# An explicit order of every engine's instructions, in place of a list scheduler, in a fused attention and spectral kernel

## The chip, the cores and the metric

The kernel runs on one core of a Trainium2 chip. The metric is device time in microseconds (us), lower is better. One program, one launch, bf16 inputs and outputs. A kernel's executions are said to be *fast* or *slow*: slow is one that took more than 1.5% longer than the fastest of the same kernel. Only fast ones enter the comparisons.

Engine names as the profile has them: PE is the matmul engine and PEld its weight loads, DVE the vector engine, ACT the scalar engine, POOL the GpSimd engine, SP the engine that issues most DMAs. "Busy" is the profile's word: matmuls overlap and their ends are modelled, so a busy PE is not PE at its peak.

## The reference, cut to what matters

Two branches over the same 2048 rows of 640, mixed by a gate per row:

```python
def _A_ref(x, wq, wk, wv, wo, beta):        # 32 heads of 20, 4 segments of 512 rows
    q, k, v = x @ wq, x @ wk, x @ wv        # split in heads and segments  [shortened]
    for s in range(4):
        p = softmax(qs @ ks.T * scale + mask)          # causal inside the segment
        a_dot = p @ vs
        a_mem = (phi(qs) @ M) / (phi(qs) @ z + 1e-06)  # memory of earlier segments
        outs.append(g * a_mem + (1 - g) * a_dot)
        M = M + phi(ks).T @ vs
        z = z + phi(ks).sum(rows)
    return concat(outs) @ wo
def _B_ref(x, w_r, w_i):
    return irfft2(rfft2(x) * (w_r + 1j * w_i))
g = sigmoid((x * gate_w).sum(-1))
out = g * A + (1 - g) * B                   # both branches on the same x
```

Both branches become matmuls in the kernel: the Fourier transforms are products with tables, and the second axis is folded first.

## The kernel before

The kernel records some 2350 operations with what they read and write, and each operation carries one or two *alternatives* (engine, function, cost, latency). Then a list scheduler runs a small clockwork of the chip on the host and decides the order in which each engine gets its instructions, and the PSUM bank that each result goes to.

The matmul helper and the evictions. All matmuls go through `mms`, so nearly all have the line number of that helper in the profile:

```python
def mms(self, items, r, w, prio, name="", extra=0.0):
    cost = sum(max(c * PECOL, 27.0) for _, c in items) + extra
    def f(e):
        for th, _ in items:
            o_, l_, r_, st, sp_, kw = th()
            h = e.matmul(o_, l_, r_, start=st, stop=sp_, **kw)
        return h
    return self.Sc.op({"pe": (f, cost, 110.0)}, r=r, w=w, prio=prio, name=name)

def either(self, fn, n, r, w, prio, name="", after=()):       # side work: DVE or POOL
    return self.Sc.op({"dve": (fn, 75 + 0.52 * n, 90.0), "pool": (fn, 100 + 1.95 * n, 90.0)}, ..., lock=True)
```

The score loop. The scores of four heads are four row-tiled matmuls that run at once in different rows of the array; they fill all four banks of the pool "qk", one exponential empties them, and only then may the next scores start. There are 80 such rounds:

```python
def qk_unit(self, s, pr, u, parts):
    bank = Bank(4, "qk")                     # the pool "qk" has 4 banks
    ...
        return (self.ps(bank, hh * 512 + o, [1, n]), kp.ap(..., p0=32 * hh, np_=DH),
                qp.ap(..., p0=32 * hh, np_=DH), True, True, {"tile_position": (32 * hh, 0)})
    ...
    self.one("act", lambda e: e.activation(dst(), src(), ACT.Exp, scale=SC), 4 * width, [bank], ...)
    # then a causal mask on POOL (affine_select), and 21-column matmuls of the probabilities with v
```

Three kinds of matmul stand in the stream: plain ones on the whole array; row-tiled scores as above; and column-tiled ones (`tile_position: (0, 32*q)`), which put four 32-column products side by side. Work beside the score loop (projections, the two transforms, memory reads, output projections) is what PE does while ACT is in an exponential.

The scheduler's heart, with cuts:

```python
def schedule(self, pools, plan=(), nsem=56):
    for o in ops if plan else ():            # PLAN: shifts of priorities, picks of alternatives
        shift, pick = divmod(plan[o.key], 3)
        o.prio += shift / 10.0
        ...
    def try_dispatch(e):                     # first ready operation by priority, banks free, not faster elsewhere
        ...
            if e == "pe":
                occ *= self.pe_slow(now, occ)
            if e == "dve" and o.lock:        # DVE and POOL share a port, in the model
                busy_until[e] = port = max(now, busy_until["pool"]) + occ
            if o.dma:                        # one number for the bandwidth of all transfers
                bw_free = max(bw_free + o.xfer, ...)
                o.t1 = bw_free + 2000.0 + lat
    while events: ...
```

The softmax here doesn't subtract the row's maximum and nothing guards it: scores larger than these inputs give would overflow.

## Time and profile before

254.12 us, median of three executions (253.64 to 255.82). The profiled execution took 255.64 us, near the top of that.

The exponentials of the kernel before: minimum, median and maximum duration in ns, the first and last start in us, then what ended ACT's idle time before them.

```profile
L1183 ACT ACTIVATE ex<-psum x80: 1857/1877/1966, 12.4 to 238.5; 128x2048 bf16<-128x2048 f32 x80
...
  PE psum L593: 17.3, 37
```

### The profile page before, as it was taken

What the parts mean: (1) busy time and instruction counts of PE and PEld (TensorE: products, weight loads), DVE (VectorE), ACT (ScalarE), POOL (GpSimd) and SP (SyncE); (2) the same over time, 40 slices, a digit from 0 to 9 for tenths busy, and PEclk for the clock granted to TensorE, in tenths of its full rate; (3) what the DMA queues carried; (4) which work ended last, traced back from release to release, by engine and by line L of the source; (5) the groups of instructions that cost most, each with busy time, mean ns of one, the idle gap of its engine ahead of it and who ended that gap; (6) DMA issues with size and microseconds to landing.
All of it is one profiled execution on the core that took longest, in us unless ns stands there. A gap on an engine that the chain in (4) does not pass through costs nothing.

```text
span 253.9 us, 7958 instructions
## 1 busy us (share of the span) xinstructions
PE 235.9 (93%) x3226; PEld 138.4 (55%) x3248; DVE 202.2 (80%) x556; ACT 203.1 (80%) x208; POOL 114.4 (45%) x175
## 2 busy tenths in 40 slices
PE   7999999989999989989989999999997999999993
PEld 2344556544665547644646566545563656456583
DVE  0789799759998899999999988979999984625543
ACT  2397499958999898999988889889889798788710
POOL 8004735523533336745255747535575532416400
PEclk9999999979999999999999999999999999999998
DMA  7997979599479366656238385313666303464223
GB/s 173 358 355 216 216 173 225 121 205 221 101 112 227 79 168 189 159 125 191 64 96 182 70 204 141 101 44 114 134 169 153 70 3 84 92 115 94 78 68 103
DMA packets 56003, 36.76 MB, mean 145 GB/s; under 512 B 31792, under 2 KB 52256, under 8 KB 55968
## 3 DMA queue, kind: packets, MB, share of 16 engines
q1 hardware_dynamic: 54272, 35.45, 57.6%
q10 hardware_dynamic: 1696, 0.82, 1.2%
q8 instruction: 25, 0.41, 0.7%
q14 instruction: 10, 0.08, 0.2%
HBM read 19.86 MB, written 9.84 MB: 117 GB/s over the span
## 4 chain that ended last, share of the span: by engine, by line
PE 57%; DVE 19%; DMA 10%; ACT 5%; SPq 3%; issue 3%; POOL 1%; ACTq 0%; DVEq 0%
PE psum L593 57%; ACT ex L1183 4%; DMA xsb<-in_A_x_dram 4%; DVE Pt L1333 3%; DMA pkn<-phk 3%; SPq L622 2%; DVE va L1089 2%; DVE xsb L913 1%; SPq L620 1%; DMA tt<-tab_tt 1%; DVE Cp L603 1%; DVE qu L603 1%; DVE xf L908 1%; DMA q_scr<-qu 1%; DMA Wt<-in_B_w_i_dram 1%
## 5 line engine op out<-in xcount | busy, mean ns | idle before, releaser
L1183 ACT ACTIVATE ex<-psum 128x2048 bf16<-128x2048 f32 x80 | 150.3, 1879 | 17.9 <-PE psum L593 17.3
L1186 POOL TENSOR_SCALAR_AFFINE_SELECT ex<-ex 128x512 bf16<-128x512 bf16 x128 | 80.7, 647 | 110.7 <-ACT ex L1183 109.3
L593 PEld LDWEIGHTS psum<-va,ex 128*128 128x128 bf16 x1280 | 36.6, 96 | 7.2 <-POOL ex L1186 2.5
L593 PE MATMUL psum<-va,ex 128*128 128x21 bf16 x1280 | 38.6, 173 | 1.7 <-POOL ex L1186 0.6
L593 PE MATMUL psum<-qp,kp 20*128 20x512 bf16 (+3 forms) x512 | 31.9, 303 | 1.5 <-ACT ex L1183 0.6
L593 PE MATMUL psum<-wv,xT 128*128 128x141 bf16 (+1 forms) x160 | 28.0, 306 | 1.5 <-DVE qu L603 0.6
L1333 DVE TENSOR_TENSOR Pt<-psum,Wt 128x642 bf16<-128x642 f32 x32 | 25.6, 822 | 2.7 <-PE psum L593 1.6
L593 PE MATMUL psum<-xT,wk 128*128 128x512 bf16 (+1 forms) x127 | 25.6, 384 | 2.1 <-DVE qu L603 0.8
L593 PE MATMUL psum<-xT,wq 128*128 128x512 bf16 (+1 forms) x132 | 26.5, 380 | 0.7 <-issue 0.4
L593 PE MATMUL psum<-wo,oT 128*128 128x320 bf16 x120 | 22.1, 301 | 0.0
L593 PEld LDWEIGHTS psum<-qp,kp 20*128 20x128 bf16 x512 | 9.0, 92 | 20.4 <-ACT ex L1183 10.7
L593 PEld LDWEIGHTS psum<-wv,xT 128*128 128x128 bf16 x160 | 13.0, 98 | 10.5 <-issue 1.2
L593 PE MATMUL psum<-big,Cp 128*128 128x321 bf16 (+1 forms) x96 | 17.2, 302 | 1.0 <-DVE eo L603 0.4
L1054 ACT ACTIVATE et<-qu 128x512 bf16<-128x512 bf16 x25 | 15.7, 635 | 2.5 <-DVE qu L603 2.4
L603 DVE CAST ot<-psum 128x320 bf16<-128x320 f32 x19 | 9.1, 490 | 10.6 <-PE psum L593 9.4
L1089 DVE TENSOR_TENSOR va<-psum,ebx 128x500 bf16<-128x500 f32 (+1 forms) x32 | 15.2, 482 | 2.8 <-PE psum L593 1.7
L593 PEld LDWEIGHTS psum<-xT,wk 128*128 128x128 bf16 (+1 forms) x140 | 9.7, 98 | 13.5 <-issue 2.7
L1379 DVE TENSOR_TENSOR G<-eo,psum 128x320 bf16<-128x320 f32 x32 | 14.7, 476 | 2.5 <-PE psum L593 2.4
L593 PEld LDWEIGHTS psum<-xT,wq 128*128 128x128 bf16 (+1 forms) x140 | 10.0, 97 | 11.3 <-issue 1.3
L1218 DVE TENSOR_TENSOR on<-psum,rs 128x320 bf16<-128x320 f32 x32 | 15.5, 483 | 0.3
L593 PE MATMUL psum<-big,Ac 128*128 128x161 bf16 (+2 forms) x96 | 14.5, 257 | 1.3 <-DVE qu L603 0.9
L593 PE MATMUL psum<-tt,Yt 128*128 128x256 bf16 (+1 forms) x96 | 15.0, 273 | 0.3
(80 smaller groups left out, 357.2 us busy)
## 6 DMA issues: line engine op xcount, KB each, us to landing
tt<-tab_tt SPq DMA_DIRECT2D x16, 256.0 KB, 2.9
xsb<-in_A_x_dram SPq DMA_DIRECT2D x8, 320.0 KB, 6.9
qp<-q_scr SPq DMA_DIRECT2D x28, 80.0 KB
kp<-k_scr SPq DMA_DIRECT2D x28, 80.0 KB
o_scr<-on SPq DMA_DIRECT2D x12, 160.0 KB
out_dram<-ot SPq DMA_DIRECT2D x12, 160.0 KB
q_scr<-qu SPq DMA_DIRECT2D x6, 256.0 KB
k_scr<-qu SPq DMA_DIRECT2D x6, 256.0 KB, 2.8
```

Source lines behind the costliest of these rows:

```text
L593: h = e.matmul(o_, l_, r_, start=st, stop=sp_, **kw)
L603: alts["dve"] = (lambda e: e.tensor_copy(dst(), src()), 75 + 1.04 * n, 85.0)
L620: return e.dma_start_transpose(d_, s_)
L622: return e.dma_start(d_, s_)
L908: self.either(lambda e, r=r, op=op: e.tensor_tensor(xf.ap(r * 642, [321, 2], [1, 320]), xs.ap(o, [D, 2], [1, 320]), xs.ap(o + 320, [D, 2], ...
L1054: self.one("act", lambda e: e.activation(et.ap(0, [1, L]), qsl(), ACT.Exp), L, [qb], [b("et", pi_)], late, name="phi_exp")
L1089: self.one("dve", lambda e: e.tensor_tensor(va.ap(i * H * VW + h0 * VW, [VW, nh], [1, DH]), self.ps(bank, 0, [DH, nh], [1, DH]), self.ebx. ...
L1183: self.one("act", lambda e: e.activation(dst(), src(), ACT.Exp, scale=SC), 4 * width, [bank], [self.exb(s, g, j) for g, j in outs], prio - ...
L1186: self.one("pool", lambda e, g=g, j=j: e.affine_select(self.ex.ap(self.exo(s, g) + JOFF[j], [1280, 4], [1, P]), self.ex.ap(self.exo(s, g) ...
L1218: self.one("dve", lambda e, rs=rs, bank=bank, g=g: e.tensor_tensor(on.ap(80 * g, [D, 4], [DH, 4], [1, DH]), self.ps(bank, 0, [88, 4], [VW, ...
L1333: self.one("dve", lambda e, ri=ri, Pt=Pt, Wt=Wt, bank=bank: e.tensor_tensor(Pt.ap(ri * 322, [644, 2], [1, KD]), self.ps(bank, 0, [0, 2], [ ...
L1379: self.one("dve", lambda e, q=q, n2=n2, bank=bank, eo=eo: e.tensor_tensor(self.G.ap(n2 * D + 639 * q, [1 - 2 * q, 320]), eo.ap(q, [1, 320] ...
```

## The change

The intent: no scheduler at all. `ORDER` lists every operation with the alternative chosen, found by a search over a more detailed model of the chip; each engine runs its queue in exactly that order. The model prices a change of tiling between matmuls and models DMA rings, issue times and late landings. Two pieces of work change too: plain matmuls may be cut in four 32-column pieces so as to stay in the column tiling of their neighbours, and a query tile whose result nobody reads is dropped.

```diff
@@ class Sched
-    def schedule(self, pools, plan=(), nsem=56):
+    COST = {(0, 1): 94.0, (0, 2): 94.0, (1, 0): 110.0, (1, 2): 110.0, (2, 0): 110.0, (2, 1): 94.0}
+    def schedule(self, pools, order, nsem=56):
         ops = self.ops
-        [ready lists, events, priorities, bandwidth: about 190 lines cut]
+        queue = {e: [] for e in self.eng}
+        for v in order:
+            o = ops[v // 2]
+            o.eng = list(o.alts)[v % 2]
+            queue[o.eng].append(o)
+        [emode: the tiling that each matmul will have; 20 lines cut]
+        while len(self.order) < len(order):
+            [take the queue head that can start first; place its banks; book its time]
+            if e == "pe" and o.emode != mode:
+                occ += self.COST[mode, o.emode]
+                mode = o.emode
@@ def mms
-        cost = sum(max(c * PECOL, 27.0) for _, c in items) + extra
+        cost = sum(c * PECOL + 0.75 if mode > 0 else max(c * PECOL + 2.8, 25.4) for _, c in items) + extra
         ...
                 o_, l_, r_, st, sp_, kw = th()
+                if op.mode < 0 and op.emode == 2:
+                    for q in range(0, m, 32):       # four pieces of 32 columns
+                        [dst, wt: the piece's output partitions and weights]
+                        h = e.matmul(dst, wt, r_, ..., **{**kw, "tile_position": (0, q), ...})
+                else:
-                h = e.matmul(o_, l_, r_, start=st, stop=sp_, **kw)
+                    h = e.matmul(o_, l_, r_, start=st, stop=sp_, **kw)
@@ def proj_tile
+        if s == 0 and which == "q" and t == 0:
+            return
@@ the matmuls of the transforms and of the output projection
-                self.mms(..., name="Db")
+                self.mms(..., name="Db", mode=-1)   # may be cut; likewise D, T, Tb and oproj
@@ class Kern
-    PLAN = ( [about 1300 shifts and picks] )
+    ORDER = ( [about 2350 entries] )
+    QUEUE = { [issue, ring work and width of every kind of DMA] }
```

The costs of the other operations in the model are adjusted as well; that touches nothing that runs on the chip, as the order is given.

## The prediction

> **What bounds the kernel now.** The page shows PE busy 93% of 253.9 us (ACT and DVE 80%, POOL 45%); the chain of waits lies 57% on PE. From starts of successive matmuls in the timeline: an untiled matmul costs its columns at 2.4 per ns plus 2.8 ns; the 21-column ones cost 25 ns; four tiled ones of 320 columns together cost 136 ns, as one untiled of 320. I estimate 204.5 us of streaming for the 3248 matmuls. Between kinds of tiling (untiled, row-tiled scores, column-tiled projections and gate products) the trace has 206 changes, each about 95 to 110 ns beyond the columns: 20.6 us. The Trainium skill, "TensorEngine Tiling (Array Packing)", Key Properties, says that changing the mode drains the engine; the trace agrees. First matmul to last is 248.4 us, so 23 remain: about 4 from half clock in the first 6.7 us and at 54 to 58 us, and 18 to 20 of stalls. By ten-microsecond windows, stalls lie at 50 to 60 (a key-feature transpose takes 7.5 us), 80 to 110, 120 to 140, 150 to 170 and 190 to 200; from 200 to 250 there are almost none, but 73 of the mode changes.
>
> **What the change does.** Nearly the same work in another order.
> 1. The dead query tile goes: 5 matmuls of 512 columns (1.1 us of PE), one eviction (0.5 us), half a store.
> 2. Reading the order list against the operations: tiling changes fall from 206 to 175, as 120 output-projection and 33 last-inverse-transform matmuls are cut in four 32-column pieces and stay in the column-tiled mode. 31 x 0.1 = 3.1 us of PE, mostly in the stall-free end, so it counts in full. The pieces cost no more: 136 against 136 ns.
> 3. Side work moves from DVE to POOL (folds 6 to 14, W additions 9 to 18, memory additions 4 to 16): at the traced 0.24 us (0.4 for folds) DVE loses some 8 us; POOL gains about 20.
> 4. Order: stalls are to shrink, as the search knew issue times and late landings. This is the uncertain term.
>
> **How much is critical.** Floor of the new order on PE: 204.5 - 1.1 + 17.5 + 3.3 (cold start) + 5.4 (before the first and after the last matmul start) = 229.6 us. ACT is a near second: exponentials cost 1.77 us start to start, and between the third and the last one ACT has about 180 us of work against 187 us on PE. Two engines 96% full that feed each other will stall; I expect 8 or 9 us: 229.6 + 8.5 = 238 us.
>
> **Prediction: 238 us, range 232.5 to 247.** Chances: faster by over 2% 0.91, within 2% 0.07, slower 0.02.
>
> **What would show it.** 175 tiling changes, few of them in the last 40 us; PE busy share 95% or more; stalls mostly under 1 us per window; the last exp near 224 instead of 238.5 us; the wait for the key-feature transpose at 50 us and its clock drop gone; DVE busy under 195 us, POOL over 130; the chain more on PE.
>
> **What would make it wrong.** The strict order waits on something the search modelled badly: start-up loads (input loads now go before the transposes; the first exp could come later than 12.4 us), or a late DMA in the middle, which stops all engines behind it: 245 or more. Or the cut matmuls' 32-column weight loads don't hide behind the columns. Or the stalls vanish wholly: 231.

## More of the kernel before

The page of the kernel before: the span, the busy time of the engines with instruction counts, two rows of tenths over 40 slices of the span (PE busy, and the clock granted to PE, where 9 is full), the instruction-fetch queue, and the chain of work that ended last, by engine and by line.

```profile
span 253.9 us, 7958 instructions
...
PE 235.9 (93%) x3226; PEld 138.4 (55%) x3248; DVE 202.2 (80%) x556; ACT 203.1 (80%) x208; POOL 114.4 (45%) x175
...
PE   7999999989999989989989999999997999999993
...
PEclk9999999979999999999999999999999999999998
...
q8 instruction: 25, 0.41, 0.7%
...
PE 57%; DVE 19%; DMA 10%; ACT 5%; SPq 3%; issue 3%; POOL 1%; ACTq 0%; DVEq 0%
```

PE is busy 93% of the span and more than half of the chain is on it. Two other engines are at 80%. In the middle the three are closer than the page's average tells. The stretches of the kernel before, with busy microseconds (and instructions) of each engine, then the granted clock, the DMA share and GB/s:

```profile
30.00:190.00 160.00, 149.49 (x2090) 90.30 (x2108) 144.30 (x398) 144.31 (x144) 78.95 (x125) 0.99 0.63 144
50.00:60.00 10.00, 8.30 (x117) 4.37 (x116) 6.27 (x18) 6.16 (x6) 2.59 (x5) 0.83 1.17 247
190.00:240.00 50.00, 48.44 (x698) 27.63 (x691) 31.66 (x90) 40.91 (x35) 21.84 (x33) 1.00 0.39 87
```

Between 30 and 190 us PE is busy 149.5 of 160 us, DVE 144.3 and ACT 144.3. After 190 us only PE is full (48.4 of 50 us). The stretch from 50 to 60 us is the worst for PE, and its clock falls there.

The trace also gives the round from exponential to exponential. I take the 77 rounds from the third exponential (30.46 us) to the last (238.54 us): 208.1 us, 2.70 us each. The shortest rounds take 2.38 us = 1.877 (exponential) + 0.055 (to the first score matmul) + 0.396 (score matmuls) + 0.051. So 77 rounds could not take less than 183 us in this form.

## The result, and the profile after

246.41 us, median of four executions (245.78 to 246.97), beside 254.23 us for the kernel before on the same chip (253.64 to 255.82). The ratio is 0.968, with a 95% interval of 0.963 to 0.974. A ratio here is the mean time of one kernel's fast runs over that of the other's of the same rounds, so not quite the ratio of the medians. The output is correct. So the sign was right; of the 16 us that I forecast, 7.8 came.

The page of the kernel after, the same rows (L498 is the plain matmul call, L496 the one of the cut pieces):

```profile
span 244.2 us, 8905 instructions
...
PE 233.1 (95%) x3702; PEld 139.8 (57%) x3702; DVE 198.8 (81%) x534; ACT 201.6 (83%) x204; POOL 132.2 (54%) x200
...
PE   7999999999999999999978999999899999999994
...
PEclk9999999999999999999999999999999999999999
...
q8 instruction: 29, 0.48, 0.8%
...
PE 72%; DVE 16%; DMA 5%; ACT 4%; issue 2%; SPq 0%; DVEq 0%
```

The stretches of the kernel after:

```profile
30.00:190.00 160.00, 154.71 (x2131) 91.33 (x2130) 146.85 (x399) 147.27 (x145) 93.83 (x147) 1.00 0.54 141
50.00:60.00 10.00, 10.00 (x159) 6.38 (x157) 8.15 (x23) 9.70 (x14) 5.70 (x10) 1.00 0.84 191
190.00:240.00 50.00, 49.30 (x1332) 35.27 (x1336) 30.55 (x80) 36.86 (x33) 23.13 (x35) 1.00 0.64 112
```

The exponentials of the kernel after:

```profile
L1137 ACT ACTIVATE ex<-psum x80: 1859/1877/1926, 13.3 to 229.7; 128x2048 bf16<-128x2048 f32 x80
...
  PE psum L498: 14.8, 36
```

Three readings.

First, what was fixed. PE is now full from 50 to 60 us and the clock no longer falls. In the profiled execution of before, DVE waited 2.2 us until 57.7 us for a transpose of key features to land, and PE's clock was at half for 3.4 us from 54.5 us, after gaps of PE at 52 and 53 us; all of that is gone. The drop of the clock belongs to that execution: six executions of before in the other rounds whose clock is recorded as 1.000 took 253.4 to 255.0 us (leaving out the disturbed one told of at the end), so it is not where most of the gain comes from. PE's changes of tiling fell from 206 to 175, as counted by walking the matmuls of the trace.

Second, what was not. From start to start of successive matmuls I can split PE's time in three terms, columns, changes of tiling (0.1 us each), and the rest (stalls, and half clock at the start and, in before, in the middle):

| us | before | after, predicted | after, measured |
|---|---|---|---|
| columns | 204.5 | 203.4 | 203.4 |
| changes of tiling | 20.6 | 17.5 | 17.5 |
| cold start and stalls | 23.3 | 11.8 | 18.4 |
| before the first and after the last matmul start | 5.4 | 5.4 | 4.9 |
| span | 253.9 | 238.1 | 244.2 |
| time beyond the span | 1.75 | not in my sum | 1.74 |

("Measured" is the profiled execution of 245.98 us. The predicted third term is 3.3 of cold start plus the 8.5 of stalls that I allowed.) Two terms are right to 0.1 us. The third is off by 6.6 us, and I compared a sum of span with a time that is 1.75 us longer than its span.

Third, where in the program the gain lies. The start of the k-th exponential says how far the program has come. In us, before minus after, and for the last line the start in the kernel after:

| exponential number | 0 | 4 | 8 | 16 | 24 | 40 | 52 | 64 | 72 | 79 |
|---|---|---|---|---|---|---|---|---|---|---|
| before minus after | -0.9 | 1.3 | 1.5 | 4.2 | 6.7 | 7.3 | 6.3 | 6.7 | 7.3 | 8.8 |
| start in after | 13 | 35 | 45 | 68 | 88 | 129 | 161 | 191 | 212 | 230 |

All of the gain comes before 88 us and after 191 us. For the hundred microseconds between, where I had counted the largest stalls of before (80 to 110, 120 to 140, 150 to 170), the new order is no faster than the old one. There the stalls moved (a stall is here the time between starts of matmuls beyond columns and changes of tiling): the trace of after has less of them at 80 to 110 us (2.3, before 4.9) and at 150 to 170 us (0.6, before 2.5), and more at 120 to 130 us (3.8, before 2.5) and at 170 to 190 us (3.3, before 1.1).

The worst place of the new order, in order of time, from the kernel after. Columns: start and length in us, engine, line, operation, and in brackets the idle time before it with what ended it:

```profile
128.21 1.51 POOL L1292 TENSOR_TENSOR Yt<-Pt 128x321 bf16<-128x321 bf16 x2 [0.77 <-DVE Pt L1287]
128.24 0.88 DVE L1292 TENSOR_TENSOR Yt<-Pt 128x321 bf16<-128x321 bf16 x1
...
129.04 0.85 DVE L1177 TENSOR_TENSOR on<-on,mem 128x320 bf16<-128x320 bf16 x1
...
129.81 0.56 DVE L1021 TENSOR_SCALAR phk<-qu 128x512 bf16<-128x512 bf16 x1
130.30 0.51 DVE L509 CAST Bt<-psum 128x322 bf16<-128x322 f32 x1
...
130.87 0.60 PE L498 MATMUL psum<-xT,wq 128*128 128x512 bf16 x2 [1.22 <-DVE Bt L509]
```

PE idles 1.22 us at 129.65 us for one eviction (Bt) which stands in DVE's queue behind an addition to `on` and a step of the feature map. Those wait for nothing: DVE is simply full, and it is longer at this work than it need be. The addition of two Pt halves took 0.88 us and the one to `on` 0.85 us, while POOL read its own operands; the same additions alone take 0.3 us.

That is a price of the third step of the change. POOL took over 9 W additions, 12 memory additions and 5 folds, and got 17.8 us more work (114.4 to 132.2). DVE's busy time became 3.4 us shorter (202.2 to 198.8), where I had expected some 8. The durations of DVE's instructions, summed one by one, did fall by 7.5 us (236.7 to 229.2). But they overlap in the trace, so that a duration taken away is not that much busy time taken away. And the W additions that remained on DVE got slower: 9 of 23 left, yet their sum fell by 1.4 us only (7.7 to 6.3). The memory additions that remained did not (428 ns on average before, 432 after). The durations of the W additions on DVE, minimum, median and maximum in ns, first before, then after:

```profile
L1338 DVE TENSOR_TENSOR Yt<-Pt x23: 268/323/495, 61.7 to 177.1; 128x321 bf16<-128x321 bf16 x23
```

```profile
L1292 DVE TENSOR_TENSOR Yt<-Pt x14: 268/324/912, 51.4 to 171.8; 128x321 bf16<-128x321 bf16 x14
```

The Trainium skill, "SBUF — State Buffer", section "Who interferes with whom", states that a DVE instruction with two SBUF inputs contends with a GpSimd instruction that reads SBUF, for a port pair that is locked exclusively. The trace agrees: the fastest of these additions takes 268 ns in both kernels, the slowest went from 495 to 912 ns, and all that took over 500 ns ran while a POOL instruction ran. The median is the same (323 and 324 ns): few are hit, but hard.

### The profile page after: what moved, and what is told of

Same layout as the page of the kernel before. It is cut to its first block, busy times and chain, and to the rows that moved or that the text cites. A ratio compares the mean times of both kernels' runs of the same rounds, so it can differ in the third digit from the quotient of the medians.

```text
span 244.2 us, 8905 instructions
## 1 busy us (share of the span) xinstructions
PE 233.1 (95%) x3702; PEld 139.8 (57%) x3702; DVE 198.8 (81%) x534; ACT 201.6 (83%) x204; POOL 132.2 (54%) x200
## 4 chain that ended last, share of the span: by engine, by line
PE 72%; DVE 16%; DMA 5%; ACT 4%; issue 2%; SPq 0%; DVEq 0%
PE psum L498 64%; PE psum L496 8%; DVE Pt L1287 4%; ACT ex L1137 3%; DMA xT<-in_A_x_dram 2%; DMA oT<-o_scr 2%; DVE Cp L509 2%; DVE Yt L1292 1%; DVE qu L509 1%; ACT et L1010 1%; DVE va L1045 1%; DVE Bt L509 1%; DVE on L1172 1%; DVE on L1177 0%; DVE phk L1021 0%
## 5 line engine op out<-in xcount | busy, mean ns | idle before, releaser
L498 PEld LDWEIGHTS psum<-va,ex 128*128 128x128 bf16 x1280 | 39.0, 96 | 5.8 <-issue 1.3
L498 PE MATMUL psum<-va,ex 128*128 128x21 bf16 x1280 | 41.1, 172 | 0.1
L498 PE MATMUL psum<-xT,wk 128*128 128x512 bf16 (+1 forms) x140 | 33.3, 380 | 0.6 <-DMA xT<-in_A_x_dram 0.6
L498 PE MATMUL psum<-xT,wq 128*128 128x512 bf16 (+1 forms) x135 | 32.2, 380 | 1.2 <-DVE Bt L509 1.2
L498 PE MATMUL psum<-qp,kp 20*128 20x384 bf16 (+3 forms) x512 | 31.7, 301 | 0.7 <-ACT ex L1137 0.2
L498 PE MATMUL psum<-wv,xT 128*128 128x500 bf16 (+1 forms) x160 | 31.9, 300 | 0.2
L496 PE MATMUL psum<-wo,oT 128*32 128x320 bf16 x480 | 23.0, 300 | 0.2 <-issue 0.2
L498 PEld LDWEIGHTS psum<-qp,kp 20*128 20x128 bf16 x512 | 9.0, 92 | 18.3 <-ACT ex L1137 9.6
L509 DVE CAST ot<-psum 128x320 bf16<-128x320 f32 x21 | 9.9, 489 | 11.6 <-PE psum L496 8.4
L498 PEld LDWEIGHTS psum<-wv,xT 128*128 128x128 bf16 x160 | 13.3, 97 | 10.0 <-DVE Ac L509 0.8
L498 PE MATMUL psum<-big,Ac 128*128 128x321 bf16 (+2 forms) x96 | 17.9, 256 | 0.8 <-DVE Cp L509 0.4
L498 PE MATMUL psum<-tt,Yt 128*128 128x256 bf16 (+1 forms) x96 | 17.0, 274 | 0.4 <-DVE qu L509 0.2
L1292 POOL TENSOR_TENSOR Yt<-Pt 128x321 bf16<-128x321 bf16 x18 | 13.4, 757 | 7.2 <-DVE Pt L1287 4.6
L509 DVE CAST qu<-psum 128x512 bf16<-128x512 f32 x20 | 13.6, 686 | 3.4 <-PE psum L498 3.2
L498 PEld LDWEIGHTS psum<-xT,wk 128*128 128x128 bf16 (+1 forms) x140 | 9.9, 97 | 10.9 <-issue 2.3
L1177 POOL TENSOR_TENSOR on<-on,mem 128x320 bf16<-128x320 bf16 x16 | 12.8, 806 | 5.8 <-DVE on L1172 5.8
```

The costliest lines, as they stand in the source:

```text
L496: h = e.matmul(dst, wt, r_, start=st, stop=sp_, **{**kw, "tile_position": (0, q), "skip_group_check": True})
L509: alts["dve"] = (lambda e: e.tensor_copy(dst(), src()), 67 + 1.04 * n, 68.0)
L1177: self.either(lambda e, g=g: e.tensor_tensor(on.ap(80 * g, [D, 4], [1, 80]), on.ap(80 * g, [D, 4], [1, 80]), self.mem.ap(80 * g, [D, 4], [ ...
L1292: fn = lambda e, r=r, a0=a0, a1=a1, op=op, Pt=Pt, Yt=Yt: e.tensor_tensor(Yt.ap(r * 322, [1, KD]), Pt.ap(a0 * 322, [1, KD]), Pt.ap(a1 * 322 ...
```

## The experiments

All were run on one core like the kernels, five rounds each beside the kernel before, four kernels to a chip. "Relief" runs take time off one engine without touching any order.

| run | what it is | median us (low to high) | ratio to before | 95% |
|---|---|---|---|---|
| e1_old_order | old order, new machinery | 254.19 (252.44 to 258.46) | 0.998 | 0.994 to 1.003 |
| e2_old_order_cut | the same, matmuls cut | 254.77 (252.84 to 257.50) | 0.999 | 0.994 to 1.004 |
| e3_new_order_uncut | new order, nothing cut | 248.47 (247.66 to 249.37) | 0.977 | 0.974 to 0.980 |
| e4_pool_to_dve | after, POOL's additions back on DVE | 248.53 (248.16 to 255.84) | 0.979 | 0.974 to 0.983 |
| r_pe | after, 10.7 us off PE | 246.30 (245.28 to 382.12) | 0.964 | 0.958 to 0.970 |
| r_exp | after, 11.2 us off the exponentials | 246.43 (246.14 to 248.93) | 0.968 | 0.962 to 0.974 |
| r_all | after, 35 us off PE, ACT, DVE | 244.62 (241.98 to 247.09) | 0.955 | 0.948 to 0.962 |
| r_gate | after, sixteen 4-element operations changed | 246.05 (245.19 to 251.03) | 0.967 | 0.959 to 0.974 |
| c_after | after, unaltered | 247.81 (246.44 to 252.12) | 0.974 | 0.969 to 0.978 |
| s1_research | another searched order | 254.76 (250.18 to 257.47) | 0.986 | 0.980 to 0.992 |
| s3_jit | another, searched with random delays | 257.67 (255.83 to 259.76) | 1.011 | 1.006 to 1.015 |
| r_all4 | after, 46 us off PE, ACT (twice), DVE | 241.52 (240.47 to 242.37) | 0.948 | 0.945 to 0.952 |
| r_act | after, 11.6 us off ACT | 246.27 (245.60 to 248.62) | 0.966 | 0.961 to 0.971 |
| r_dve | after, 12.9 us off DVE | 245.70 (244.26 to 251.87) | 0.962 | 0.957 to 0.968 |
| r_pe_exp | after, r_pe and r_exp together | 245.77 (244.81 to 247.16) | 0.963 | 0.958 to 0.968 |
| e5_evict_first | after, one DVE instruction moved | 246.23 (245.23 to 252.48) | 0.963 | 0.958 to 0.968 |

The medians and ranges are over all six executions, slow ones too. The two measurements of the unaltered kernel after differ by 0.5% (0.968 and 0.974), on two chips, so a difference under 0.5% between runs of different calls says nothing.

### What the parts of the change are worth: e1, e2, e3, e4

The question: does the order give most of the gain, or do the tiling and the placing of side work? The expectations name the theories by letters and say what each is. e1 feeds the order that the old scheduler had made to the new machinery, without cuts; e2 is e1 with the cuts allowed; e3 is the new kernel with no cuts; e4 is the new kernel with 18 W additions and 16 memory additions back on DVE at the same places.

```diff
# e1 and e3: nothing is cut
-            o.emode = o.mode
-            if o.mode < 0:
+            o.emode = max(o.mode, 0)
+            if False:
# e1 and e2: the old order (without the dead tile)
-    ORDER = (the searched order)
+    ORDER = (what the scheduler of before decided, operation by operation)
# e4: in ORDER, 34 entries take the DVE alternative
```

e1_old_order, expected:

> The order of the kernel before (each engine's own sequence), emitted by the new machinery, without the dead query tile, no matmul cut: 208 tiling changes. If the prediction's terms 1 is right and the machinery itself (bank and semaphore choice) is worth nothing, this is 1 us under before: 253 us, between 252 and 254. If the machinery or the dead tile were the source of the gain: 247 to 250.

e2_old_order_cut, expected:

> e1 with the cut into 32-column pieces (120 output projections and 15 of the last inverse transform): tiling changes fall from 208 to 183. If 25 changes count in full at 0.1 us: 2.5 us under e1. If the cut is hidden by other waits, under 1 us. If the pieces' weight loads do not hide: slower than e1.

e3_new_order_uncut, expected:

> The new order with nothing cut: 200 tiling changes against 175. If the cut counts in full: 2.5 us over the changed kernel (246.4), so 249. The order then explains the rest, about 4 us of the 7.8. If the order is worth nothing by itself, this is 251 or more; if the cut is worth nothing, 246.4.

e4_pool_to_dve, expected:

> The new order with the 18 W additions and 16 memory additions that it gives to POOL put back on DVE at the same places. Theory A (stalls are built into an order with PE, ACT and DVE all near full; the move to POOL relieved DVE): DVE gets 34 x 0.24 = 8 us more in a strict order, 4 to 8 us slower, 250 to 254. Theory B (the move cost the expected gain: POOL holds the SBUF port that DVE's two-input operations need, so DVE lost as much as it gained): within 1.5 us of the changed kernel, 245 to 248, and DVE operations with two SBUF inputs back near their shortest times (additions 0.30 us, maximum 0.27 us).

Measured: 254.19, 254.77, 248.47 and 248.53 us. The new list is worth some 5.5 us (254.19 to 248.47 by the medians, 2.1% by the ratios, on the same chip). That is order and the placing of side work together, as e3 has both; e4, below, puts the placing at 1 to 2.5 us of it, so that the order alone is worth some 3 to 4.5 us (an estimate, the difference of the two). The dead tile and the greedy placing of banks are worth nothing that these rounds resolve: e1 is 0.2% under before, within the interval. The cuts are worth 1 to 2 us in the new order (0.977 against 0.968 and 0.974, the two measurements of the change on other chips; the interval of the second overlaps that of e3) and nothing in the old one (0.998 and 0.999), though e2 has 25 changes of tiling less than e1 (183 and 208, counted in the orders). The exponentials of e3 start within 0.2 us of those of after up to number 64, at 191 us; in the last 16 rounds e3 falls 2.7 us behind. That is the stretch where PE alone is full, and there a change of tiling costs what the trace says it costs. I had predicted 3.1 us for 31 changes; e3 has 25 more than after. Why the same cut shows nothing in the time of the old order is open: in the profiles the last 16 rounds of e2 are 1.4 us shorter than those of e1, but its earlier ones are longer.

With the additions back on DVE the kernel is 1 to 2.5 us slower (0.979 against 0.968 and 0.974). So the move to POOL pays, though less than the 8 us that I took off DVE. The time lies between what the two theories of the expectation said (250 to 254, and 245 to 248). In its profile the exponential number 64 starts 1.7 us later than in after; what it loses behind that is mostly a stall at 212 us and half clock after it (see the end).

### Which engine is the floor: r_pe, r_exp, r_all, r_gate

My prediction had called the PE sum the floor. The rival was the round of scores and exponential, whose minimum of 183 us lies close to PE's work. Each relief run shortens some operations of one engine by a known amount and leaves the order, the waits and all other work as they are; the result is wrong where a table or a projection is cut short. r_exp and r_act, below, still came within the comparison's tolerance.

```diff
# r_pe: three of the five contraction steps of the value projection become 16 columns wide (wrong result)
-            self.mms([(lambda c=c: (self.ps(bank, 0, [1, w]), ...
+            self.mms([(lambda c=c, w=w if c in (0, 4) else 16: (self.ps(bank, 0, [1, w]), ...
# r_exp: 70 of 80 exponentials read 192 of 2048 columns less
+            wx = width if s == 0 and pr < 2 else width - 48
-            dst = lambda: self.ex.ap(o0, [1280, 4], [1, width])
+            dst = lambda: self.ex.ap(o0, [1280, 4], [1, wx])        # src likewise
# r_all: r_pe, and on ACT 28 of 30 feature-map exponentials of 16 columns, and on DVE the W products of 100 columns
-            ... ACT.Exp), L, [qb], [b("et", pi_)],
+            ... over nx = L if self.phc < 2 else 16 columns
-                    Pt.ap(ri * 322, [644, 2], [1, KD]), ...
+                    Pt.ap(ri * 322, [644, 2], [1, nw]), ...         # nw = KD if g < 2 else 100
# r_gate: 16 four-element DVE operations of the gate become reciprocals (one input; wrong result)
-        e.tensor_tensor(sl(self.om), sl(self.gi), sl(self.gr), ALU.mult)
+        e.reciprocal(sl(self.om), sl(self.gi))                      # three more of this kind
```

r_pe, expected:

> The changed kernel in its own order, with 10.7 us taken off the tensor engine (three of the five value-projection matmuls of each group cut to 16 columns; result wrong on purpose). Theory P, that of the prediction (PE is the limit, the rest are stalls of the order): the time falls by most of it, 8 to 11 us, to 236 to 238. Theory C (PE, the loop score matmul - exp - score matmul, and DVE are all near critical, and a strict order hands over from one to another): 0 to 3 us, 243.5 to 246.5.

r_exp, expected:

> The changed kernel with each exp from the 11th on 192 of its 2048 columns shorter (160 ns less, 70 times: 11.2 us off ACT and off the loop score matmul - exp - score matmul; result wrong on purpose). If the loop alone sets the pace: 8 to 11 us faster, 236 to 238. Theory P: ACT is not the limit, 0 to 1 us. Theory C: 0 to 3 us, 243.5 to 246.5.

r_all, expected (the text speaks of the exponentials too, but the kernel that ran does not have r_exp's edit; r_all4 further down has it):

> All reliefs at once: PE 10.7 us, exps 11.2 us, the key and query exps on ACT 11.6 us, the filter products on DVE 12.9 us (wrong on purpose). Theory P: no more than r_pe. Theory C: clearly more than the sum of r_pe and r_exp if only PE, ACT and DVE are near critical (6 to 10 us faster, 236 to 240); about 3 us if DMA issue, POOL and landings are near critical too.

r_gate, expected:

> The changed kernel with its 16 four-element gate operations on DVE that read two SBUF operands, or copy and add within SBUF, made reciprocals of one operand (wrong on purpose), which the traces show never stretched by a running POOL instruction. In the changed kernel's trace these operations take up to 0.73 us instead of 0.15 where they meet a POOL instruction, and DVE is without a gap from 114 to 131 us, where PE then stalls for 3.8 us. If that stall comes from the shared port: 1.5 to 2.5 us faster, 244 to 245, and stalls in 120 to 132 down to about 1.5 us. If not: within 0.5 us.

Measured: r_pe 246.30, r_exp 246.43, r_all 244.62, r_gate 246.05 us. That PE is the floor falls: 10.7 us off it bought one per cent at most. That the round is the floor falls as well: 11.2 us off the exponentials bought 0.6% at most (0.968 against 0.968 and 0.974). The relief of PE lies between 23 and 167 us, so it tests the floor there, and not in the last 50 us. The profile of r_pe fell in an execution of 382 us and can't be used (more of it at the end). That of r_exp shows plainly where its relief went. Three rounds in order of time, score matmuls on PE and exponentials on ACT, first from the kernel after, then from r_exp:

```profile
57.12 1.89 ACT L1137 ACTIVATE ex<-psum 128x2048 bf16<-128x2048 f32 x1
...
59.11 0.40 PE L498 MATMUL psum<-qp,kp 20*128 20x384 bf16 x8
...
59.56 1.88 ACT L1137 ACTIVATE ex<-psum 128x2048 bf16<-128x2048 f32 x1
...
61.49 0.40 PE L498 MATMUL psum<-qp,kp 20*128 20x256 bf16 x8
...
61.94 1.88 ACT L1137 ACTIVATE ex<-psum 128x2048 bf16<-128x2048 f32 x1
...
63.99 0.40 PE L498 MATMUL psum<-qp,kp 20*128 20x512 bf16 x4
...
64.50 1.87 ACT L1137 ACTIVATE ex<-psum 128x2048 bf16<-128x2048 f32 x1
```

```profile
57.00 1.72 ACT L1139 ACTIVATE ex<-psum 128x1856 bf16<-128x1856 f32 x1
...
59.15 0.40 PE L498 MATMUL psum<-qp,kp 20*128 20x384 bf16 x8
...
59.59 1.72 ACT L1139 ACTIVATE ex<-psum 128x1856 bf16<-128x1856 f32 x1 [0.17 <-PE psum L498]
...
61.46 0.40 PE L498 MATMUL psum<-qp,kp 20*128 20x256 bf16 x8
...
61.91 1.72 ACT L1139 ACTIVATE ex<-psum 128x1856 bf16<-128x1856 f32 x1
...
63.96 0.39 PE L498 MATMUL psum<-qp,kp 20*128 20x512 bf16 x4
...
64.44 1.70 ACT L1139 ACTIVATE ex<-psum 128x1856 bf16<-128x1856 f32 x1
```

The exponentials are 0.16 us shorter, and the score matmuls start where they started, within 0.04 us: they stand in PE's queue behind other matmuls, which had no reason to go faster. Over all 77 rounds the wait from the end of an exponential to the next score matmul grew from 0.28 to 0.44 us on average, by just the 0.16 us that were taken off, and the sum of the rounds stayed at 202 us (202.1 and 202.4).

The r_gate run concerns the place shown above. Four-element operations on DVE had been stretched from 0.15 to 0.73 us by POOL. With one input and less to fetch, the exponentials from number 40 on start 1.2 us earlier in the profile; in the time it is not resolved (246.05 us, interval of the ratio 0.959 to 0.974). The stalls of PE between 120 and 132 us fell from 3.8 to 2.8 us, not to the 1.5 that I expected, so the stretched operations are a part of that stall.

### Can the order be improved by search: c_after, s1_research, s3_jit, and all reliefs at once: r_all4

c_after is the kernel after again, as a control. s1_research and s3_jit are new `ORDER` lists: I annealed the order with the kernel's own cost model, to which I added the lock between DVE and POOL for the gate operations; s3_jit also with random delays. r_all4 is r_all with r_exp's edit.

```diff
# s1_research, s3_jit: correct results
-    ORDER = (the order of after)
+    ORDER = (an order that the altered model holds to be shorter)
```

c_after, expected:

> The changed kernel once more, unaltered, as a control on the chip of the other runs of this batch: ratio 0.968 to before within 0.005, some 246.4 us.

s1_research, expected:

> The changed kernel with another order only, searched from its order by annealing over its own cost model, to which one thing was added: the gate operations of DVE wait for a running POOL instruction, as the traces show. If the remaining stalls are a matter of order (slack can still be found with the same work on every engine): 1.5 to 4 us faster than the changed kernel, 242.5 to 245. If the changed order is at the limit of the engines' coupling, or the gain fits only the model: 245.5 or more.

s3_jit, expected:

> As the other new order, but searched as the mean of two draws of random delays of up to 80 ns after each operation, so that it should tolerate small deviations. If orders fail on the chip by such deviations, this beats the other new order; I expect 243 to 246, and the difference under 1.5 us.

r_all4, expected:

> What the text of r_all said and that kernel was not: r_all had the cuts on PE (10.7 us), on the key and query exps of ACT (11.6 us) and on DVE (12.9 us), and not the shorter score exps. This one has those too (11.2 us more off ACT and off the score loop). If the score loop held r_all back: 3 us or more under r_all, 241.5 or less. If the strict order with DVE, POOL and the unrelieved last 80 us holds it: within 1.5 us of r_all, 243 to 246.

Measured: 247.81, 254.76, 257.67 and 241.52 us. The control is a little above what I expected (0.974, where I had said 0.968 within 0.005). Both new orders are slower than the one that they started from, though I had expected a gain; four of the six executions of s1_research were slow ones, and the two fast ones (250.18 and 251.87 us) are still 1.2% behind c_after by the ratios. In their profiles, that of s1_research from a slow execution, PE is at half clock for 10.2 us (s1_research) and 13.7 us (s3_jit) after 127 us, which the model knows nothing of. If half clock costs half of these stretches, that is some 5 and 7 us (an estimate) of the 8.6 and 10 us by which their profiled spans exceed that of after. A search over the model does not carry over by itself.

r_all4 takes 10.7 us from PE, 22.8 us from ACT and 12.9 us from DVE, 46 us in all, and gains 6.3 us on the unaltered kernel of the same rounds by the medians (5.1 us if the other measurement of it, 0.968, is taken). For 46 us of work less over three engines that is little. Whether the shorter score exponentials added anything to r_all is not clear: 3.1 us by the medians, on two chips, but 0.2 us between the profiled executions (241.98 and 241.80). What is left, near 240 us, is the start, the end and the hand-overs of an order that does not move.

The profiled execution of c_after was a slow one, and shows something else. The matmuls of c_after around 210 us:

```profile
209.99 0.44 PE L496 MATMUL psum<-wo,oT 128*32 128x320 bf16 x7
214.86 1.76 PE L496 MATMUL psum<-wo,oT 128*32 128x320 bf16 x21 [4.43 <-issue]
216.18 0.71 PE L496 MATMUL psum<-big,Cp 128*32 128x321 bf16 x4
```

"issue" says that PE waited for nothing that the profile shows. In the trace, the queue that brings instructions (q8; by its count of packets, 25 before and 29 with the cuts, it serves PE) starts a transfer at 210.62 us, in this gap. In the fast profile of the same kernel that transfer, the 22nd, starts at 205.44 us. Half clock followed from 214.80 to 218.21 us, and the last exponential came 6.2 us later than in the other profile of the same kernel. More of it below.

### Single and paired reliefs, and a repair: r_act, r_dve, r_pe_exp, e5_evict_first

What was open: whether ACT beside the exponentials, or DVE, is the floor, or PE and the exponentials together; or none of these, as all hand over in a fixed order. e5_evict_first is no relief but a correct kernel: the eviction of Bt at 130 us goes ahead of the memory addition.

```diff
# r_act: the feature-map exponentials of r_all alone;  r_dve: its W products alone
# r_pe_exp: the edits of r_pe and r_exp
# e5_evict_first: in ORDER, entry 1569 (the eviction) moves up past six entries, the memory addition (2580) among them
-        ..., 1562, 1552, 1564, 2580, 1566, 2942, 2882, 1558, 2656, 1569, 1483, ...
+        ..., 1562, 1552, 1564, 1569, 2580, 1566, 2942, 2882, 1558, 2656, 1483, ...
```

r_act, expected:

> The changed kernel with 28 of the 30 key and query exps on ACT cut to 16 columns (11.6 us off ACT, none of it in the score loop itself; wrong on purpose). If ACT's load were the limit: 6 us or more faster. Theory C: 0 to 2 us, 244.5 to 247.

r_dve, expected:

> The changed kernel with 28 of the 32 filter products on DVE cut to 200 of 642 columns (12.9 us off DVE; wrong on purpose). DVE has no gap from 114 to 131 us and PE stalls on it there. If DVE's load were the limit: 6 us or more faster. Theory C: 0.5 to 3 us, 243.5 to 246.

r_pe_exp, expected:

> r_pe and r_exp together: 10.7 us off PE and 11.2 us off the score exps; each alone moved nothing. If these two are the pair that hold each other: most of what r_all4 gained, 4 us or more under the changed kernel, 242.5 or less. If DVE is the third: 0.5 to 2.5 us, 244 to 246.

e5_evict_first, expected:

> The changed kernel with one instruction moved: on DVE the eviction for which PE waits longest (1.2 us of idle PE at 130 us) goes ahead of a memory addition that needs not be early. Correct result. If waits of PE add up to the time: 1 to 1.3 us faster, 245.2. Theory C, that the next engine's wait takes over: within 0.7 us of the changed kernel, and the later exps start less than 0.7 us earlier than in its trace.

Measured: 246.27, 245.70, 245.77 and 246.23 us, with intervals that overlap that of the change as first measured (0.963 to 0.974). The starts of the exponentials against those of after, in us (profiled executions, all fast; minus is earlier), say more. In that of r_act PE was at half clock from 199.87 to 203.28 us, so its last column is not the relief's:

| exponential number | 8 | 24 | 36 | 40 | 44 | 64 | 79 |
|---|---|---|---|---|---|---|---|
| r_exp (ACT -11.2) | 0.0 | -0.3 | 0.0 | -0.2 | -0.4 | -0.3 | 0.4 |
| r_act (ACT -11.6) | 0.0 | 0.0 | -0.1 | -0.2 | -0.2 | -0.2 | 2.6 |
| r_pe_exp (PE -10.7, ACT -11.2) | -0.5 | -0.5 | -0.1 | -0.4 | -0.1 | -0.1 | 0.6 |
| r_dve (DVE -12.9) | 0.1 | -0.1 | -0.3 | -1.3 | -1.7 | -1.8 | -0.9 |
| r_all (PE, ACT, DVE: -35) | -0.5 | -1.2 | -1.8 | -2.8 | -3.1 | -4.2 | -4.0 |
| r_all4 (PE, ACT, DVE: -46) | -0.6 | -1.7 | -2.2 | -3.4 | -3.9 | -5.4 | -4.6 |
| e5_evict_first | 0.0 | 0.1 | 0.1 | 0.1 | -0.6 | -0.6 | -0.6 |

ACT and PE together, 21.9 us lighter, get nowhere in these starts (by the time 0.5 to 1.1%, on a chip where after itself was not run). DVE alone gains at one place, 118 to 141 us, the knot shown above, and only there. Of what was run, only r_all and r_all4, where all three are lighter, gain along the whole stretch of the reliefs (those on PE and DVE end at 167 and 170 us); behind it they gain no more. DVE together with PE alone, or with ACT alone, was not run, so that it takes all three is not shown. That PE was truly relieved, and idle for it, shows in r_pe_exp, where the matmuls of the value projection are busy for 21.5 us in place of 31.9, and in this stretch:

```profile
30.00:190.00 160.00, 149.86 (x2130) 88.76 (x2130) 147.09 (x399) 139.46 (x145) 95.97 (x148) 1.00 0.55 142
```

Against the kernel after (154.71), PE is busy 4.9 us less of these 160, and ACT 7.8 us less (139.46, after 147.27), while DVE is as full as it was (147.09 and 146.85). Split into the terms of the table above, the whole run has 10.7 us less of columns than after and 11.3 us more of cold start and stalls: all that was taken off PE came back as time in which PE waited.

e5_evict_first did what it should at its place: the matmuls of PE follow each other without the gap of 1.22 us, and the exponentials after it start 0.6 us earlier, half of what was taken away. In the time it doesn't show (246.23 us; ratio 0.963 against 0.968 and 0.974; its interval overlaps the first of these, and ends just short of the second, on another chip). It is correct, and the best of my correct kernels, but that it beats the change is not shown.

## Why the prediction was right or wrong

*The sign and the tiling: right.* The changes of tiling fell to 175 as read from the list, and gave 17.5 us as forecast. The Trainium skill, "TensorEngine Tiling (Array Packing)", section "Key Properties", states that a change of the tiling mode drains the engine; the trace agrees, at about 0.1 us each. That the saving lies in the stall-free end and counts there in full was right as well: 2.7 us by the exponentials of e3 against after, 1 to 2 us by the time, 3.1 forecast. That holds for the new order only; in the old one the cut does not show (e2). The columns came out at 203.4 us, without the dead tile's 1.1; in the time the dead tile is not resolved (e1). Of the signs that I had named, PE 95%, POOL over 130 us, the chain more on PE and the wait and the clock drop near 55 us gone came true. The last exponential did not (229.7 us, 224 forecast), nor did DVE (198.8 us, under 195 forecast), and 30 changes of tiling are left in the last 40 us, where I had said few.

*The step that failed is "How much is critical", its stall term.* I took the floor of the new order on PE (229.6 us) and allowed 8 or 9 us of stalls on top, because "two engines 96% full that feed each other will stall". Measured: cold start and stalls are 18.4 us in place of 11.8; with a cold start as forecast, stalls of some 15 us in place of 8.5. These 6.6 us are most of the 7.9 us by which the profiled execution (245.98 us) missed the sum. In its place the runs show this:

1. There are three full engines, not two. DVE is busy 146.9 of the 160 us between 30 and 190 us, ACT 147.3, PE 154.7. I had counted DVE as a sink of savings only, and named ACT alone as a near second, though the page had both at 80%.
2. None of the three is the floor in the stretch where they were relieved, up to some 170 us. With the order fixed, 10.7 us off PE, 11 us off ACT in two ways, 12.9 us off DVE, or PE and ACT together each change the time by about 1% or less (ratios of 0.962 to 0.968; the unaltered kernel has 0.968 and 0.974). Time taken from one engine turns into a wait on that engine at the next hand-over, as the three rounds of r_exp show line by line, and as 11.3 us more of waiting against 10.7 us less of columns show for PE in r_pe_exp. Even 46 us over all three give only 5 to 6 us.
3. So a sum of one engine's work is not a floor to which a search gets close. Between 88 and 191 us the new order, for all its search, is level with the old one. Its gain is at the ends: the start (1.5 us by exponential number 8), the repaired place at 50 to 60 us and what follows to 88 us, and the tiling after 191 us.

*A smaller step that failed: "DVE loses some 8 us".* Its busy time fell by 3.4 us. I had added up durations that overlap, counted 8 folds where the trace has 5, and not thought of POOL stretching those operations of DVE that have two SBUF inputs. The move was still worth 1 to 2.5 us (e4).

*Forgotten: 1.75 us.* I summed the span, and compared it with a time. In the profiled execution of before the time was 1.75 us longer than the span, which the data at hand would have told me. It makes up 1.7 of the 7.9 us.

*The range.* 246.4 lies inside 232.5 to 247, near its end.

What stays open: how what is left in r_all4 splits among the hand-overs; which waits took up PE's relief, one by one, as the only profile of r_pe was of a disturbed execution; and what DVE with one other engine would give. That none of the three engines is the floor is shown for this order only, and after 191 us, where PE alone is full, no relief was tried on PE; the two other orders that I tried were slower, so whether a better order exists is not known.

## What to carry to other kernels

When three engines are each over 90% full in a stage and hand over to each other in a fixed order, don't add up one of them and call the sum a floor: take the stall time of before, ask stage by stage which of its waits the change removes, and count only those. A cheap test is relief: shorten one engine's operations without touching the order, and see whether the time follows; if it does not for any one of them, relieve them together, and look for places where all are late together, such as an eviction behind stretched side work. Savings in a stage where one engine alone is full counted at close to their full size in the new order here, and they are the ones to forecast with the most confidence.

## What the Trainium skill lacked or had wrong

- "TensorEngine Tiling (Array Packing)", "Key Properties", says that changing the mode drains PE but gives no price: these traces have about 0.1 us per change beyond the columns (206 changes, 20.6 us; after, 175 and 17.5 us). It doesn't say either that a 128-column matmul of 320 rows of output cut in four 32-column pieces costs no more than the whole (136 ns for both here), so that a matmul can take on its neighbours' mode for nothing but instructions.
- "Runtime: NRT & Kernel Launch", "Instruction fetch mechanics", calls the cost of fetching the next block of instructions mostly hidden, and names no stall of PE in code without branches. Here, with the cut matmuls (3702 weight loads in place of 3248 in the traces, 29 fetch packets in place of 25), PE stood idle, waiting for nothing that the profile shows, for 4.43 us in c_after and 2.12 us in e4_pool_to_dve. Each time a fetch (at 210.62 and 211.35 us) began within 0.3 us of the start of the gap, 7.3 and 7.8 us after the one before it; in the fast profile of the unaltered kernel this fetch came 3.6 us after its predecessor. It occurs in some executions and not in others: those of c_after and e5_evict_first lie between 245.2 and 252.5 us, those of e3_new_order_uncut, without cuts, between 247.7 and 249.4. That the fetch is the cause is argued from its place in time, not shown by a run; and s1_research has such a gap of 2.17 us at 229.1 us with no fetch in it.
- "TensorE: Matmul & The Clock Gate", "Why this matters for your kernels", advises against idle gaps of more than about 3 us. Here much shorter ones were followed by half clock: 2.12 us in e4_pool_to_dve (half clock from 213.32 to 216.73 us), and in before no gap above 0.63 us, with PE 75% busy over the 3.4 us up to the drop at 54.45 us. A gap of 1.22 us at 129.65 us in after was followed by none, so the length of a gap alone does not decide. The length of the half-clock stretch, 3.41 us, agrees with the window that the page states in Part 1.
- The same page has no state in which a whole execution is slow at a full recorded clock: one execution of the kernel before (411.7 us) and one of r_pe (382.1 us) ran at about 0.6 of the usual speed, with full clock in the records throughout; in the latter's profile the 512-column matmuls took 660 ns in place of 380, while exponentials and DVE operations took their usual time.
- "SBUF — State Buffer", "Who interferes with whom", is right about DVE with two SBUF inputs. How much it costs the small ones is not there: a product of four elements with two SBUF inputs took 150 ns at best and 669 ns at worst in the kernel after, and a cast of four elements, with one input, 108 and 731 ns.
